# First loads by quarters of D, and half of the first token block transposed by DMA, in a GeGLU feed-forward kernel

## Chip, cores and metric

One core of one Trainium2 chip. The metric is the device time of one execution in microseconds (us). A verdict is a ratio: the mean time of one kernel's fast runs over the mean of the other's fast runs of the same rounds, so it is not quite the ratio of the medians that are quoted beside it. Beside the time each run has a span, from the first to the last instruction, which is 1.7 to 2.6 us shorter (mostly 1.8) and excludes what lies around the program.

## The reference

```python
B, S, D, F = 1, 2048, 1024, 3584      # bf16 inputs
def reference(x, w_gate, w_up, w_down):
    return (gelu(x @ w_gate) * (x @ w_up)) @ w_down    # gelu: tanh approximation
```

## The kernel before

The kernel works on two halves of the tokens. D lies on the partitions for the first two products, so x is needed transposed, as `xT`, in 8 tiles (kd = 0 to 7) of 128 rows of D; a token block is 512 tokens. The first 512 columns of w_gate and w_up (four groups of 128, "units") are done with 128 plain bf16 matmuls, the "first phase" here. All that follows is done in groups of seven products with prepared sums, the "second phase" (line 396, then 632); it keeps TensorE busy to the end.

The start of the first half, cut:

```python
XQ = 512; NSU = 3; NWARM = 11
load_x0_piece(0)                         # SP: 512 tokens x 512 of D, 512 KB
load_w((0, 0), 0, 2, nc.scalar)          # ACT: tiles 0,1 of w_gate, then w_up, 256 KB each
# ... 11 warm-up matmuls on constants ...
load_x0_piece(1)                         # SP: the other half of D
for k0 in range(2, 8, 2):
    load_w((0, 0), k0, k0 + 2, nc.sync)  # SP: tiles 2 to 7, full 512 columns
load_xT(xT, 0, 1, 0, KD)                 # SP: 2nd token block, one DMA transpose of 8 tiles
load_w((0, 1), 0, KD, nc.sync)           # SP: the next chunk of columns

def first_units(hT):
    # warm-up, 16 TensorE transposes (kd 0..3), then per kd six matmuls:
    # three units are held open at once; before kd = 3 the other 16 transposes
    ...
# then unit 3 of block 0, and units 0 to 3 of block 1, banks in rotation
```

Of the kernel before, what the change touches and what calls it, by code (L numbers as in the profile page):

```python
# [34 lines left out]
def kernel(  # L35
# [9 lines left out]
    P = 128  # L45
# [13 lines left out]
    DN = 512  # L59
    NDN = D // DN  # L60
    TSB = TB // P
    XQ = 512
    NXQ = D // XQ
    KPQ = XQ // P
    WKP = 2
    NSU = 3
    NWARM = 11
    NPAIR = KF // 2
    PPG = FPG // 2
    WDT = 2  # L70
# [36 lines left out]

    banks = [psum.tile([P, TB], F32, name=f"bank{i}") for i in range(8)]
    PB, VB, QB, RB = (0, 1), (2, 3), (4, 5), (6, 7)
    bank_ctr = [0]  # L110

    def next_bank():
        b = banks[bank_ctr[0] % 8]
        bank_ctr[0] += 1
        return b

    last_on = {}

    def on(engine, inst):
# [8 lines left out]
    def sp(inst):  # L128
        return on("sp", inst)
# [4 lines left out]
    def dve(inst):  # L134
        return on("dve", inst)
# [25 lines left out]
            for j in range(2)  # L161
        )

    def load_w(key, k0, k1, eng):
        c0 = key[1] * FG
        for w_sb, wv in zip(chunks[key], (wgv, wuv)):
            i = eng.dma_start(out=w_sb[:, k0:k1, :], in_=wv[:, k0:k1, c0 : c0 + FG])  # L167
            if eng is nc.sync:
                sp(i)

    def load_x0_piece(q):
        sp(
            nc.sync.dma_start(
                out=xs0[:, :, q * XQ : (q + 1) * XQ],
                in_=x2[0:TB, q * XQ : (q + 1) * XQ].rearrange(
                    "(ts p) d -> p ts d", p=P
                ),
            )
        )

    def load_xT(xT, h, tb, k0, k1):
        t0 = h * SH + tb * TB
        sp(
            nc.sync.dma_start_transpose(
                out=xT[:, k0:k1, tb * TB : (tb + 1) * TB],
                in_=xv[t0 : t0 + TB, k0:k1, :],
            )
        )

    xT = xT_pool.tile([P, KD, SH], BF16, name="xT")  # L190
    new_chunk((0, 0))
    load_x0_piece(0)
    load_w((0, 0), 0, WKP, nc.scalar)
    nc.scalar.preload_act_table(ACT.Gelu_apprx_tanh)
    ident = const_pool.tile([P, P], BF16, name="ident")
    make_identity(nc, ident[:])

    warm_l = nc.const_aps.tensor(1.0, [P, P], BF16)
    warm_r = nc.const_aps.tensor(1.0, [P, TB], BF16)
    warm = []  # L200
    for i in range(NWARM):
        b = banks[i % 8]
        warm.append(
            nc.tensor.matmul(b[:], lhsT=warm_l, rhs=warm_r, start=True, stop=True)
        )

    load_x0_piece(1)
    for k0 in range(WKP, KD, WKP):
        load_w((0, 0), k0, k0 + WKP, nc.sync)
    load_xT(xT, 0, 1, 0, KD)  # L210
    new_chunk((0, 1))
    load_w((0, 1), 0, KD, nc.sync)


    tsum = {}
# [25 lines left out]


    def mm_gu(ps, w_sb, fi, tb, kd):
        return nc.tensor.matmul(  # L244
            ps[:],
            lhsT=w_sb[:, kd, fi * P : (fi + 1) * P],
            rhs=xT[:, kd, tb * TB : (tb + 1) * TB],
            start=(kd == 0),
            stop=(kd == KD - 1),
        )  # L250

    g_ctr = [0]
# [19 lines left out]
            )  # L272
        )

    def unit(hT, key, fi, tb):
        pss = (next_bank(), next_bank())
        for ps, w_sb in zip(pss, chunks[key]):
            for kd in range(KD):
                mm_gu(ps, w_sb, fi, tb, kd)
        mult(hT, gelu(pss[0]), pss[1], key[1] * FPG + fi, tb)  # L280

    evac_ctr = [0]

    def evac(dst, src):
        if evac_ctr[0] % 2 == 0:
            dve(nc.vector.tensor_copy(out=dst, in_=src))
        else:
            act(nc.scalar.copy(out=dst, in_=src))
        evac_ctr[0] += 1

    def transpose_x_piece(q):
        kds = list(range(q * KPQ, (q + 1) * KPQ))
        parts = []
        if q == 0:
            parts = [([kds[0]], (0, 2)), ([kds[0]], (2, 4)), ([kds[1]], (0, 4))]
            kds = kds[2:]
        parts += [(kds[i : i + 2], (0, 4)) for i in range(0, len(kds), 2)]
        insts = []
        for kd_list, (ts0, ts1) in parts:
            n = (ts1 - ts0) * P  # L300
            tp = next_bank()[:].bitcast(BF16)
            for j, kd in enumerate(kd_list):
                for ts in range(ts0, ts1):
                    c = j * n + (ts - ts0) * P
                    insts.append(
                        nc.tensor.transpose(  # L306
                            tp[:, c : c + P],
                            xs0[:, ts, kd * P : (kd + 1) * P],
                            ident[:],
                        )  # L310
                    )
            k0 = kd_list[0]
            evac(
                xT[:, k0 : k0 + len(kd_list), ts0 * P : ts1 * P],
                tp[:, 0 : len(kd_list) * n].rearrange("p (a b) -> p a b", b=n),
            )
        return insts

    def first_units(hT):
        groups = [warm, transpose_x_piece(0)]  # L320
        held = [(banks[2 + 2 * u], banks[3 + 2 * u]) for u in range(NSU)]
        bank_ctr[0] = 0
        for kd in range(KD):
            if kd == KPQ - 1:
                bank_ctr[0] = 0
                groups.append(transpose_x_piece(1))
            g = []
            for j, w_sb in enumerate(chunks[(0, 0)]):
                g += [mm_gu(held[u][j], w_sb, u, 0, kd) for u in range(NSU)]
            groups.append(g)  # L330
        for ga, gb in zip(groups[:-1], groups[1:]):
            tc.add_manual_dep(
                gb[0].ins, ga[-1].ins.name, SCHED_DEP, reason="startup PE order"
            )
        t_sum("t1")
        for u in range(NSU):
            mult(hT, gelu(held[u][0]), held[u][1], u, 0)
        bank_ctr[0] = 0


    ssum = {}
# [434 lines left out]
    for h in range(NH):  # L776
        hT = hT_pool.tile([P, KF, SH], BF16, name="hT")
        first_pair = 0
        if h == 0:
            first_units(hT)  # L780
            t_sum("t2")
            for fi in range(NSU, FPG):
                unit(hT, (0, 0), fi, 0)
            t_sum("b22")
            t_sum("t3")
            unit(hT, (0, 0), 0, 1)
            for name in S_NAMES:
                for j in range(2):
                    s_sum(0, PPG, j, name)
            t_sum("t4")  # L790
            for fi in range(1, FPG):
                unit(hT, (0, 0), fi, 1)
            first_pair = PPG
            xs = [(tb, kd) for tb in range(NTB) for kd in range(KD)]
            stage_load(0)
            stage_load(1)
        for pair in range(first_pair, NPAIR):
            if pair % PPG == 0 and (pair // PPG + 1) * PPG < NPAIR:
                key = (h, pair // PPG + 1)
                if key not in chunks:  # L800
                    new_chunk(key)
                    load_w(key, 0, KD, nc.sync)
            then = {}
            if h == 0:

# [44 lines left out]
        if h + 1 < NH:  # L850
            nh = h + 1
            xT = xT_pool.tile([P, KD, SH], BF16, name="xT")

            def x_fill(k0, k1):
                src = x_dram[:, k0:k1, :]
                sp(nc.sync.dma_start(out=xT[:, k0:k1, :], in_=src))

            def w_fill(c, j):
                if j == 0:
                    new_chunk((nh, c))  # L860
                w_sb, wv = chunks[(nh, c)][j], (wgv, wuv)[j]
                for k0 in range(0, KD, KH):
                    src = wv[:, k0 : k0 + KH, c * FG : (c + 1) * FG]
                    sp(nc.sync.dma_start(out=w_sb[:, k0 : k0 + KH, :], in_=src))

            def s_fill(j, *names):
                for name in names:
                    s_sum(nh, 0, j, name, True)

            then0["m6"] = [  # L870
                lambda k0=k0: x_fill(k0, k0 + WKP) for k0 in range(0, KD, WKP)
            ]
            then1["m6"] = [lambda: w_fill(0, 0)]
            then1["m7"] = [lambda: w_fill(0, 1)]
            then1["m2"] = [
                lambda: s_fill(0, "s1"),
                lambda: s_fill(1, "s1"),
                lambda: s_fill(0, "s2"),
                lambda: s_fill(1, "s2"),
                lambda: s_fill(0, "s3"),  # L880
                lambda: s_fill(1, "s3"),
            ]
            then1["m3"] = [lambda: t_sum("t1")]
            then1["m4"] = [
                lambda: s_fill(0, "a22"),
                lambda: s_fill(1, "a22"),
                lambda: t_sum("b22"),
                lambda: t_sum("t2"),
                lambda: t_sum("t3"),
                lambda: s_fill(0, "s4"),  # L890
                lambda: s_fill(1, "s4"),
                lambda: t_sum("t4"),
                pool_behind_dve,
                lambda: [w_fill(1, j) for j in range(2)],
            ]
# [32 lines left out]
```

## Time and profile before

| | before |
|---|---|
| time, median of 6 runs | 545.12 us (544.7 to 546.16) |
| span of the profiled run | 542.7 us |
| TensorE busy | 99% of the span |
| first real matmul | 6.41 us |
| second phase starts | 35.53 us |

The prediction below shows the chain and the timeline, columns start, length, engine, line, what. Two more lines, of the list of waits (who waited, for whom: us in total, times, longest), first 40 us:

```profile
PE bank L244 <- DMA w_mem<-in_w_up_dram: 0.4, 1, 0.4
...
SPq L184 <- DMA w_mem<-in_w_up_dram: 1.5, 1, 1.5
```

The first is TensorE's only wait after its first matmul. The second is the load queue on SP: before it issues the DMA transpose of line 184 it waits for an earlier load of w_up to land. The dates fit eight completion semaphores used in turn, so that a DMA waits for the one eight places before it; this is inferred from which loads are waited for. One line of the timeline, columns start, length, engine, line, what:

```profile
37.22 4.03 PE L396 MATMUL bank<-t_mem,s_mem 128*128 128x512 f32 x16
```

The second phase's first eight plain matmuls start at 35.53, and the first product with prepared sums at 37.22 us, 1.69 us later.

### The profile page before, as it was taken

The numbers are of one execution on the slowest core, as the hardware profiler recorded it, in microseconds if no ns is written. First come the engines' busy times: TensorE is split into PE (matmuls) and PEld (weight loads), VectorE is DVE, ScalarE is ACT, GpSimd is POOL, SyncE is SP. The second block draws the span as 40 slices with busy tenths as digits, with TensorE's granted clock in tenths as the row PEclk, the third lists the DMA queues.
The fourth block names the chain that finished last, engine by engine and source line by source line (L and its number), as shares of the span: only waits on it lengthen the run. The fifth ranks groups of instructions, "written<-read, shape, count | busy, mean of one in ns | idle before, by whom it ended". The sixth has DMA issues, their size and how long they took to land.

```text
span 542.7 us, 7261 instructions
## 1 busy us (share of the span) xinstructions
PE 537.7 (99%) x2411; PEld 374.1 (69%) x2411; DVE 349.5 (64%) x465; ACT 259.8 (48%) x434; POOL 242.2 (45%) x206
## 2 busy tenths in 40 slices
PE   8999999999999999999999999999999999999997
PEld 4456677777767676767777766777766776866865
DVE  1826666778766899789484444444454469979961
ACT  2435555555555318216455555555555552462270
POOL 0577777888877000000038776677777630000000
PEclk9999999999999999999999999999999999999999
DMA  9845598877736979679962240404040457767845
GB/s 275 267 133 155 162 241 278 216 252 194 252 137 213 335 246 367 215 245 307 320 213 80 76 129 27 155 2 156 0 156 0 156 171 238 251 219 246 289 146 206
DMA packets 81669, 104.82 MB, mean 193 GB/s; under 512 B 16608, under 2 KB 63200, under 8 KB 81632
## 3 DMA queue, kind: packets, MB, share of 16 engines
q1 hardware_dynamic: 81088, 103.83, 60.0%
q10 hardware_dynamic: 544, 0.52, 0.3%
q8 instruction: 20, 0.33, 0.2%
q14 instruction: 17, 0.14, 0.1%
HBM read 87.56 MB, written 13.63 MB: 186 GB/s over the span
## 4 chain that ended last, share of the span: by engine, by line
PE 98%; DMA 1%; ACT 0%; ACTq 0%; issue 0%
PE bank L396 60%; PE bank L632 32%; PE bank L244 5%; DMA w_mem<-in_w_up_dram 1%; PE bank L306 0%; ACT o_sb L680 0%; ACTq L167 0%; ACTq L680 0%
## 5 line engine op out<-in xcount | busy, mean ns | idle before, releaser
L396 PE MATMUL bank<-t_mem,s_mem 128*128 128x512 f32 x1016 | 249.2, 399 | 0.0
L396 PEld LDWEIGHTS bank<-t_mem,s_mem 128*128 128x128 f32 x1016 | 190.9, 188 | 44.2
L370 POOL TENSOR_TENSOR s_mem<-w_mem 128x512 fp32r<-128x512 bf16 x100 | 120.9, 1230 | 196.1 <-DVE t_mem L238 105.0
L632 PE MATMUL bank<-t_mem,s_mem 128*128 128x512 f32 x560 | 130.1, 392 | 0.0
L419 DVE TENSOR_TENSOR bank<-bank,m 128x512 f32<-128x512 f32 x104 | 72.3, 699 | 81.3 <-ACT bank L439 72.3
L632 PEld LDWEIGHTS bank<-t_mem,s_mem 128*128 128x128 f32 x560 | 105.2, 188 | 22.7
L267 DVE TENSOR_TENSOR hT<-w_mem,bank 128x512 bf16<-128x512 f32 x104 | 71.3, 688 | 54.4 <-ACT w_mem L262 24.6
L262 ACT ACTIVATE w_mem<-bank 128x512 f32<-128x512 f32 x104 | 61.9, 597 | 79.4 <-DVE bank L419 46.2
L396 PE MATMUL bank<-xT,w_mem 128*128 128x512 bf16 x416 | 99.0, 380 | 0.0
L396 PEld LDWEIGHTS <-w_mem 128*128 128x128 bf16 x416 | 36.6, 98 | 50.5 <-issue 13.6
L545 DVE TENSOR_TENSOR t_mem<-w_mem 128x1024 fp32r<-128x1024 bf16 x56 | 65.5, 1216 | 0.0
L370 POOL TENSOR_TENSOR s_mem<-w_mem,s_mem 128x512 fp32r<-128x512 bf16 x50 | 63.3, 1288 | 0.0
L370 POOL TENSOR_TENSOR s_mem<-s_mem,w_mem 128x512 fp32r<-128x512 f32 x50 | 59.3, 1206 | 0.0
L607 DVE TENSOR_TENSOR s_mem<-hT 128x512 fp32r<-128x512 bf16 x56 | 40.5, 754 | 10.5 <-PE bank L632 7.0
L383 ACT CAST s_mem<-w_mem 128x512 fp32r<-128x512 bf16 x52 | 31.9, 615 | 30.4 <-PE bank L396 29.2
L632 PEld LDWEIGHTS <-hT 128*128 128x128 bf16 x224 | 21.3, 98 | 26.6 <-issue 1.8
L434 ACT COPY m<-bank 128x512 f32<-128x512 f32 x52 | 30.6, 589 | 17.2 <-PE bank L396 17.0
L439 ACT COPY bank<-bank 128x512 f32<-128x512 f32 x52 | 29.6, 570 | 17.1 <-PE bank L396 17.1
L430 ACT COPY bank<-bank 128x512 f32<-128x512 f32 x52 | 29.5, 570 | 13.4 <-PE bank L396 13.4
L680 ACT CAST o_sb<-bank 128x512 bf16<-128x512 f32 x28 | 15.4, 586 | 39.6 <-PE bank L632 39.6
L244 PE MATMUL bank<-xT,w_mem 128*128 128x512 bf16 x128 | 28.1, 379 | 0.4 <-DMA w_mem<-in_w_up_dram 0.4
L542 ACT CAST t_mem<-w_mem 128x1024 fp32r<-128x1024 bf16 x28 | 26.9, 1048 | 0.0
(39 smaller groups left out, 233.4 us busy)
## 6 DMA issues: line engine op xcount, KB each, us to landing
t_mem<-t_dram SPq DMA_DIRECT2D x56, 512.0 KB, 5.5
w_mem<-in_w_gate_dram SPq DMA_DIRECT2D x11, 1024.0 KB, 6.2
w_mem<-in_w_up_dram SPq DMA_DIRECT2D x11, 1024.0 KB, 8.4
wd_sb<-in_w_down_dram SPq DMA_DIRECT2D x28, 256.0 KB, 3.4
t_dram<-o_sb SPq DMA_DIRECT2D x28, 256.0 KB, 2.5
wd_sb<-in_w_down_dram SPq DMA_DIRECT2D x12, 512.0 KB, 8.5
w_mem<-in_w_down_dram SPq DMA_DIRECT2D x10, 512.0 KB, 5.8
w_mem<-in_w_down_dram SPq DMA_DIRECT2D x4, 1024.0 KB, 6.8
```

The source lines that it names most:

```text
L244: return nc.tensor.matmul(ps[:], lhsT=w_sb[:, kd, fi * P : (fi + 1) * P], rhs=xT[:, kd, tb * TB : (tb + 1) * TB], start=(kd == 0), stop=(k ...
L262: act(nc.scalar.activation(out=g_sb, in_=ps[:], func=ACT.Gelu_apprx_tanh))
L267: nc.vector.tensor_tensor(out=hT[:, fc, tb * TB : (tb + 1) * TB], in0=g_sb, in1=ps[:], op=ALU.mult,)
L370: pool(nc.gpsimd.tensor_tensor(out=t, in0=in0, in1=in1, op=op))
L383: act(nc.scalar.copy(out=t, in_=a(1, 1)))
L396: nc.tensor.matmul(banks[bank][:], lhsT=lhs[:, c, :], rhs=rhs[:, c, :], start=start and c == 0, stop=c == KH - 1, skip_group_check=True,)
L419: nc.vector.tensor_tensor(out=banks[dst][:], in0=banks[src][:], in1=m5[j][:], op=ALU.add)
L434: act(nc.scalar.copy(out=m5[j][:], in_=banks[VB[j]][:]))
L439: act(nc.scalar.copy(out=banks[RB[j]][:], in_=banks[QB[j]][:]))
L545: dve(nc.vector.tensor_tensor(out=t, in0=in0, in1=in1, op=ALU.subtract))
L607: dve(nc.vector.tensor_tensor(out=t, in0=in0, in1=in1, op=op))
L632: nc.tensor.matmul(banks[bset[u]][:], lhsT=lhs(i, u), rhs=rhs(i), start=start and i == 0, stop=stop and i == NS - 1, skip_group_check=True,)
```

## The change

The intent is to let TensorE begin sooner: a quarter of x and half the weight columns are enough for the first matmuls, and half of the transposing is taken off TensorE. The rest of the diff keeps instruction order fixed on each engine and changes which PSUM banks the first units use. The diff, cut to its core:

```diff
-    XQ = 512
+    XQ = 256
-    NSU = 3
-    NWARM = 11
+    NWARM = 8
@@ loads
-    load_x0_piece(0)
-    load_w((0, 0), 0, WKP, nc.scalar)
+    FA = 2 * P                                  # 256 of the 512 columns
+    load_x0(0, sp)                              # 256 KB
+    load_w(first, 0, 0, 2, act, 0, FA)          # w_gate, 128 KB
+    load_w(first, 1, 0, 2, sp, 0, FA)           # w_up
+    load_x0(1, act)
+    load_w(first, 0, 2, 4, sp, 0, FA)
+    load_w(first, 1, 2, 4, act, 0, FA)
@@ after the warm-up
-    load_x0_piece(1)
-    for k0 in range(WKP, KD, WKP):
-        load_w((0, 0), k0, k0 + WKP, nc.sync)
-    load_xT(xT, 0, 1, 0, KD)
+    for j in range(2):
+        load_w(first, j, KH, KD, sp, 0, FA)
+    for kd in range(KH, KD):
+        load_xT(xT, 0, 0, kd, kd + 1)           # four DMA transposes, block 0
+    for j in range(2):
+        load_w(first, j, 0, KD, sp, FA, FG)     # the other 256 columns
+    for k0 in range(0, KD, KH):
+        load_xT(xT, 0, 1, k0, k0 + KH)
@@ first units: two held instead of three; 8 transposes, 6 matmuls,
@@ 8 transposes, 26 matmuls; then units 2 and 3, then block 1, whose
@@ last unit now ends in banks VB, not PB
```

"Columns" below are the loads of the other 256 columns.

More of the change, by code (lines that the diff above doesn't have):

```diff
@@ L109 @@
     PB, VB, QB, RB = (0, 1), (2, 3), (4, 5), (6, 7)
-    bank_ctr = [0]
-    def next_bank():
-        b = banks[bank_ctr[0] % 8]
-        bank_ctr[0] += 1
-        return b
     last_on = {}
@@ L162, in new_chunk, with load_w, load_x0 @@
         )
-    def load_w(key, k0, k1, eng):
+    def load_w(key, j, k0, k1, queue=sp, f0=0, f1=FG):
         c0 = key[1] * FG
-        for w_sb, wv in zip(chunks[key], (wgv, wuv)):
-            i = eng.dma_start(out=w_sb[:, k0:k1, :], in_=wv[:, k0:k1, c0 : c0 + FG])
-            if eng is nc.sync:
-                sp(i)
-    def load_x0_piece(q):
-        sp(
-            nc.sync.dma_start(
-                out=xs0[:, :, q * XQ : (q + 1) * XQ],
-                in_=x2[0:TB, q * XQ : (q + 1) * XQ].rearrange(
-                    "(ts p) d -> p ts d", p=P
-                ),
-            )
-        )
+        eng = nc.scalar if queue is act else nc.sync
+        src = (wgv, wuv)[j][:, k0:k1, c0 + f0 : c0 + f1]
+        queue(eng.dma_start(out=chunks[key][j][:, k0:k1, f0:f1], in_=src))
+    def load_x0(q, queue):
+        eng = nc.scalar if queue is act else nc.sync
+        cols = slice(q * XQ, (q + 1) * XQ)
+        src = x2[0:TB, cols].rearrange("(ts p) d -> p ts d", p=P)
+        queue(eng.dma_start(out=xs0[:, :, cols], in_=src))
     def load_xT(xT, h, tb, k0, k1):
@@ L191 @@
     new_chunk((0, 0))
-    load_x0_piece(0)
-    load_w((0, 0), 0, WKP, nc.scalar)
-    nc.scalar.preload_act_table(ACT.Gelu_apprx_tanh)
+    FA = 2 * P
+    first = (0, 0)
+    load_x0(0, sp)
[4 more added lines that the diff above has]
+    load_w(first, 1, 2, 4, act, 0, FA)
+    act(nc.scalar.preload_act_table(ACT.Gelu_apprx_tanh))
     ident = const_pool.tile([P, P], BF16, name="ident")
@@ L199 @@
     warm_r = nc.const_aps.tensor(1.0, [P, TB], BF16)
-    warm = []
     for i in range(NWARM):
-        b = banks[i % 8]
-        warm.append(
-            nc.tensor.matmul(b[:], lhsT=warm_l, rhs=warm_r, start=True, stop=True)
-        )
-    load_x0_piece(1)
-    for k0 in range(WKP, KD, WKP):
-        load_w((0, 0), k0, k0 + WKP, nc.sync)
-    load_xT(xT, 0, 1, 0, KD)
+        pe(
+            nc.tensor.matmul(
+                banks[i][:], lhsT=warm_l, rhs=warm_r, start=True, stop=True
+            )
+        )
+    for j in range(2):
[6 more added lines that the diff above has]
+        load_xT(xT, 0, 1, k0, k0 + KH)
     new_chunk((0, 1))
-    load_w((0, 1), 0, KD, nc.sync)
+    for j in range(2):
+        load_w((0, 1), j, 0, KD)
     tsum = {}
@@ L243, in mm_gu @@
     def mm_gu(ps, w_sb, fi, tb, kd):
-        return nc.tensor.matmul(
-            ps[:],
-            lhsT=w_sb[:, kd, fi * P : (fi + 1) * P],
-            rhs=xT[:, kd, tb * TB : (tb + 1) * TB],
-            start=(kd == 0),
-            stop=(kd == KD - 1),
+        pe(
+            nc.tensor.matmul(
+                ps[:],
+                lhsT=w_sb[:, kd, fi * P : (fi + 1) * P],
+                rhs=xT[:, kd, tb * TB : (tb + 1) * TB],
+                start=(kd == 0),
+                stop=(kd == KD - 1),
+            )
         )
@@ L273, in mult, with unit_out, unit @@
         )
-    def unit(hT, key, fi, tb):
-        pss = (next_bank(), next_bank())
-        for ps, w_sb in zip(pss, chunks[key]):
+    def unit_out(hT, bset, fi, tb):
+        mult(hT, gelu(banks[bset[0]]), banks[bset[1]], fi, tb)
+    def unit(hT, bset, fi, tb):
+        for b, w_sb in zip(bset, chunks[first]):
             for kd in range(KD):
-                mm_gu(ps, w_sb, fi, tb, kd)
-        mult(hT, gelu(pss[0]), pss[1], key[1] * FPG + fi, tb)
-    evac_ctr = [0]
-    def evac(dst, src):
-        if evac_ctr[0] % 2 == 0:
-            dve(nc.vector.tensor_copy(out=dst, in_=src))
-        else:
-            act(nc.scalar.copy(out=dst, in_=src))
-        evac_ctr[0] += 1
@@ L291, in transpose_x_piece @@
-    def transpose_x_piece(q):
-        kds = list(range(q * KPQ, (q + 1) * KPQ))
-        parts = []
-        if q == 0:
-            parts = [([kds[0]], (0, 2)), ([kds[0]], (2, 4)), ([kds[1]], (0, 4))]
-            kds = kds[2:]
-        parts += [(kds[i : i + 2], (0, 4)) for i in range(0, len(kds), 2)]
-        insts = []
-        for kd_list, (ts0, ts1) in parts:
-            n = (ts1 - ts0) * P
-            tp = next_bank()[:].bitcast(BF16)
-            for j, kd in enumerate(kd_list):
-                for ts in range(ts0, ts1):
-                    c = j * n + (ts - ts0) * P
-                    insts.append(
-                        nc.tensor.transpose(
-                            tp[:, c : c + P],
-                            xs0[:, ts, kd * P : (kd + 1) * P],
-                            ident[:],
-                        )
-                    )
-            k0 = kd_list[0]
-            evac(
-                xT[:, k0 : k0 + len(kd_list), ts0 * P : ts1 * P],
-                tp[:, 0 : len(kd_list) * n].rearrange("p (a b) -> p a b", b=n),
-            )
-        return insts
@@ L319, in first_units @@
-    def first_units(hT):
-        groups = [warm, transpose_x_piece(0)]
-        held = [(banks[2 + 2 * u], banks[3 + 2 * u]) for u in range(NSU)]
-        bank_ctr[0] = 0
-        for kd in range(KD):
-            if kd == KPQ - 1:
-                bank_ctr[0] = 0
-                groups.append(transpose_x_piece(1))
-            g = []
-            for j, w_sb in enumerate(chunks[(0, 0)]):
-                g += [mm_gu(held[u][j], w_sb, u, 0, kd) for u in range(NSU)]
-            groups.append(g)
-        for ga, gb in zip(groups[:-1], groups[1:]):
-            tc.add_manual_dep(
-                gb[0].ins, ga[-1].ins.name, SCHED_DEP, reason="startup PE order"
-            )
-        t_sum("t1")
-        for u in range(NSU):
-            mult(hT, gelu(held[u][0]), held[u][1], u, 0)
-        bank_ctr[0] = 0
+                mm_gu(banks[b], w_sb, fi, tb, kd)
@@ new lines, in unit, with transpose_x0 @@
+        unit_out(hT, bset, fi, tb)
+    def transpose_x0(q):
+        parts = [(2 * q, 0, 4), (2 * q + 1, 0, 4)]
+        if q == 0:
+            parts = [(0, 0, 2), (0, 2, 4), (1, 0, 4)]
+        for n, (kd, ts0, ts1) in enumerate(parts):
+            tp = banks[(PB + QB)[(2 * q + n) % 4]][:].bitcast(BF16)
+            for ts in range(ts0, ts1):
+                pe(
+                    nc.tensor.transpose(
+                        tp[:, ts * P : (ts + 1) * P],
+                        xs0[:, ts, kd * P : (kd + 1) * P],
+                        ident[:],
+                    )
+                )
+            cols = slice(ts0 * P, ts1 * P)
+            if n % 2 == 0:
+                dve(nc.vector.tensor_copy(out=xT[:, kd, cols], in_=tp[:, cols]))
+            else:
+                act(nc.scalar.copy(out=xT[:, kd, cols], in_=tp[:, cols]))
@@ new lines, in first_units @@
+    def first_units(hT):
+        wg, wu = chunks[first]
+        held = (VB, RB)
+        transpose_x0(0)
+        for q in range(NXQ):
+            for kd in (2 * q, 2 * q + 1):
+                for u in range(2):
+                    mm_gu(banks[held[u][0]], wg, u, 0, kd)
+            for kd in (2 * q, 2 * q + 1):
+                for u in range(2):
+                    mm_gu(banks[held[u][1]], wu, u, 0, kd)
+                if kd == 0:
+                    transpose_x0(1)
+        for u in range(2):
+            unit_out(hT, held[u], u, 0)
@@ L780 @@
             first_units(hT)
+            unit(hT, PB, 2, 0)
+            t_sum("t1")
+            unit(hT, QB, 3, 0)
             t_sum("t2")
-            for fi in range(NSU, FPG):
-                unit(hT, (0, 0), fi, 0)
             t_sum("b22")
+            unit(hT, VB, 0, 1)
             t_sum("t3")
-            unit(hT, (0, 0), 0, 1)
             for name in S_NAMES:
@@ L789 @@
                     s_sum(0, PPG, j, name)
+            unit(hT, RB, 1, 1)
             t_sum("t4")
-            for fi in range(1, FPG):
-                unit(hT, (0, 0), fi, 1)
+            unit(hT, QB, 2, 1)
+            unit(hT, VB, 3, 1)
             first_pair = PPG
@@ L801 @@
                     new_chunk(key)
-                    load_w(key, 0, KD, nc.sync)
+                    for j in range(2):
+                        load_w(key, j, 0, KD)
             then = {}
@@ L860, in w_fill @@
                     new_chunk((nh, c))
-                w_sb, wv = chunks[(nh, c)][j], (wgv, wuv)[j]
                 for k0 in range(0, KD, KH):
-                    src = wv[:, k0 : k0 + KH, c * FG : (c + 1) * FG]
-                    sp(nc.sync.dma_start(out=w_sb[:, k0 : k0 + KH, :], in_=src))
+                    load_w((nh, c), j, k0, k0 + KH)
             def s_fill(j, *names):
```

## The prediction

> **What bounds the kernel now.** I read the page's busy table first, then the chain of waits with its list in order of time, then the timeline of the first 37 us, and last the DMA rate in 1 us stretches.
>
> ```profile
> PE 537.7 (99%) x2411; PEld 374.1 (69%) x2411; DVE 349.5 (64%) x465; ACT 259.8 (48%) x434; POOL 242.2 (45%) x206
> PE 98%; DMA 1%; ACT 0%; ACTq 0%; issue 0%
> ```
>
> TensorE is busy 99% of the span and is 98% of the chain that ended last: nothing but matmul time counts. The chain in order of time shows the only place where something else sets the end:
>
> ```profile
> 1.24 6.36 DMA w_mem<-in_w_up_dram
> 7.60 0.05 issue
> 7.65 3.41 PE bank L244 x15
> 11.06 0.89 PE bank L306 x16
> 11.95 23.74 PE bank L244 x110
> 35.70 151.35 PE bank L396 x672
> ```
>
> From 7.65 us on TensorE never stops; 110 matmuls in 23.74 us are 0.2158 us each. The start is 7.65 us of waiting for a first piece of w_up, with few matmuls before it. The timeline shows what TensorE and the load queue do there:
>
> ```profile
> 0.77 4.42 PE L204 MATMUL bank<-const-bfloat16-1.0 128*128 128x512 bf16 x11 [0.77 <-PEq L912]
> 5.51 1.07 PE L306 MATMUL bank<-ident,w_mem 128*128 128x128 bf16 x16 [0.32 <-DMA w_mem<-in_x_dram]
> 6.41 0.82 PE L244 MATMUL bank<-xT,w_mem 128*128 128x512 bf16 x3
> 7.62 6.00 SPq L184 DMA_TRANSPOSE xT<-in_x_dram  x1
> 7.65 3.41 PE L244 MATMUL bank<-xT,w_mem 128*128 128x512 bf16 x15 [0.41 <-DMA w_mem<-in_w_up_dram]
> 10.90 1.06 PE L306 MATMUL bank<-ident,w_mem 128*128 128x128 bf16 x16
> 35.53 2.04 PE L396 MATMUL bank<-xT,w_mem 128*128 128x512 bf16 x8
> ```
>
> Eleven warm-up matmuls, 16 transposes, three matmuls, a wait, then the stream. The first phase (the 128 plain matmuls of the first weight chunk) gives way to the second at 35.53 us. Only that date can move. From there to the end, some 507 us, the loop is untouched and has no wait.
>
> The DMA side, columns: stretch, length, busy time of PE, PEld, DVE, ACT, POOL, clock, DMA share, GB/s:
>
> ```profile
> 2.00:3.00 1.00, 1.00 (x4) 0.44 (x3) 0.00 (x0) 1.00 (x1) 0.00 (x0) 1.00 0.74 225
> 8.00:9.00 1.00, 1.00 (x7) 0.44 (x5) 0.00 (x0) 0.00 (x0) 0.00 (x0) 1.00 1.10 347
> 14.00:15.00 1.00, 1.00 (x6) 0.44 (x5) 0.00 (x0) 0.00 (x0) 0.00 (x0) 1.00 1.27 290
> ```
>
> Bytes flow from about 2 us on, then at 347 GB/s for plain pieces and 290 GB/s while x is transposed; the engines are full until 15.5 us. So the start is a race between fixed bytes and TensorE, and what counts is the order of the bytes.
>
> **What the Trainium skill says.** "TensorE: Matmul & The Clock Gate", section "Wait — 56ns, not 53.3ns?": 512-column matmuls start every 426.7 ns cold and every 215.7 ns warm, 128-column ones every 55.6 ns warm. The trace agrees: 0.2158 us per matmul, 0.89 us for 16 transposes, and warm-up weight loads 0.43 us apart until about 4.6 us. The same page, "What's actually happening": full clock comes after a busy window of about 3.4 us. The trace agrees roughly: warm-up began at 0.77 us and the spacing shortened at about 4.7 us. "DMA: Bandwidth & Descriptors", "Issuing engines are not separate DMA queues": a second issuing engine saves sequencer time only. The trace agrees that the total stays near 350 GB/s with both queues at work (between 4 and 8 us one moved 1.11 MB, the other 0.35). The same page, "Latency and other measured facts": 261 GB/s effective for a DMA transpose; the trace has 290.
>
> **The change part by part.**
>
> Warm-up: 8 instead of 11. 8 x 0.427 = 3.4 us, so it ends at 4.2 us instead of 5.2. It saves only if x is there by then.
>
> First x: a quarter of D, 256 KB instead of 512 KB. In the kernel before, 512 KB on the SP queue were usable at 5.5 us, when that queue had moved 0.78 MB, so landing trails the bytes by about 0.8 us. The queue had moved 0.08 MB at 2.5 us and then 0.23 MB per us. It passes 256 KB at about 3.2 us, so the piece is usable at about 4.1 us, as the warm-up ends. The first w_gate piece is 128 KB instead of 256 KB, on the ACT queue (0.11 MB per us): about 3.8 us. Both are in time.
>
> Transposes on TensorE: 16 instead of 32, in two sets of 8. The instruction order of the changed kernel puts 8 before the first matmul and 8 after the sixth. 16 x 0.056 = 0.9 us of TensorE time goes. First matmul: transposes at 4.25, plus half a tile transposed and copied by ScalarE (0.37 us for 128x256). In the kernel before, that ScalarE copy ended at 6.31 after a start at 5.51, so the first matmul could not come before 0.8 us; hence 5.1 us here instead of 6.41.
>
> Without any wait the first phase then ends at 5.1 + 128 x 0.2158 + 8 x 0.056 = 33.2 us, which is 2.4 us before 35.53. This is the ceiling.
>
> Now the waits. With no stall TensorE wants, by the same 0.2158: the second x quarter at 6.4, w_up of tiles 2 and 3 at 8.1, the four DMA-transposed tiles of x at 8.9, 9.4, 10.7 and 11.1, the other half of the columns of w_gate at 12.4 and of w_up at 14.1, and the second token block at 19.3 us.
> - Second x quarter: it ends 384 KB on the ACT queue, 2.5 + 0.36/0.11 = 5.8 us; about in time. w_up tiles 2 and 3: 512 KB on that queue, about 7.3 us; in time.
> - DMA transposes: SP issues five loads first (about 0.5 us each), then each transpose must find its completion semaphore free, which the order view shows as a wait on an earlier load (the second x quarter for the third transpose, about 6 us). In the long loop a one-tile transpose holds the SP queue 1.16 us at least, 1.67 us in the median, 4.19 us at most. From 4.0 us, four at 1.2 to 1.7 end between 8.8 and 10.8 us. Landing took 2.6 us at least, and 1.5 MB of loads ahead of them drain until about 7 us. Estimate: tiles at about 8.6, 9.8, 11.2 and 12.3 against 8.9, 9.4, 10.7 and 11.1. The last is late by some 1.2 us.
> - Other column half: issued only behind the transposes, at 9 to 11 us; about 1.4 us to first bytes (0.74 to 2.1 at the start), 1.5 us for 512 KB, 0.8 us to land: 12.7 to 14.7 against 12.4. Late by 0.3 to 2.3, largely the same wait as the one before, not added to it.
> - Second token block: two issues of 3 us (half of the 6.00), landed by about 18 to 19; in time.
>
> I book 1.0 us of wait for the transposes and columns. The clock may still be half for the transposes and first matmuls; 0.1 us more is for that. 2.4 - 1.1 = 1.3 us gained: 545.26 - 1.3 = 543.9 us.
>
> **The rivals.**
> - The ceiling: transposes land in time and the whole 2.4 us stay, 542.9 us. For it: 1.16 us issues exist, and the sizes look matched to these dates. Against: eight tiles in one instruction took 6.00 us to issue and 8.2 to land, with the DMA full.
> - The DMA transpose becomes the new wait: at 2 to 2.6 us per issue, as in the loop just behind two 1 MB loads (a pair took 5.19 us), the last tile is there at about 14 us and the columns at about 16. The gain is gone: 545 to 546.5 us.
> - The clock is not released after only 3.4 us of warm-up, and 3.4 us more of half speed follow: some 8 matmuls lost, 1.7 us, so about 545.5 us. Against: all work follows without a gap if x lands at 4.1.
> - GpSimd becomes the bound. It waits for the second weight chunk (20.24 us before) and makes the sums that TensorE wants 1.9 us into the second phase. Now the chunk is issued at 16 to 17 us instead of 13.67, landing at about 23 and 25. GpSimd had finished its first two pairs 10.5 us after its start, and the second pair is wanted at about 38 us, so some 3 us of slack stay. Otherwise the second phase stalls a few us. I give this little.
>
> **Range and chances.** Ceiling 542.9 with 0.3 us for run to run (544.74 to 545.34 before): low end 542.6. All the gain lost: 545.4. A change of 2% is 10.9 us; the whole start is 7.65 us of waiting, so faster by 2% cannot be, and slower would need waits three times any estimate above. Faster 0.005, within 0.985, slower 0.01.
>
> **What would show it.** Right: warm-up ends at about 4.2, first real matmul near 5.1, 16 identity matmuls in all, and TensorE's second phase starting near 34.2 with gaps totalling about 1 us, each ended by a DMA of xT or w_gate before 15 us. Wrong: a first matmul after 5.6 (landing is not set by bytes), transposes holding SP over 2 us each, matmul spacing of 0.43 us after 5.2, or a wait of TensorE for s_mem near 36 us.

## The result, and the profile after

| | before | predicted | changed |
|---|---|---|---|
| time, median | 545.12 us | 543.9 us | 543.59 us (543.35 to 543.98, 6 runs) |
| ratio | | | 0.9971 (0.9958 to 0.9984) |
| span of the profiled run | 542.7 | | 541.7 us |
| x usable, first transpose | 5.51 | 4.1 to 4.25 | 4.76 us |
| first real matmul | 6.41 | 5.1 | 5.62 us |
| identity matmuls | 32 | 16 | 16 |
| time of the first phase after that without matmul or transpose | 0.60 | 1.0 | 0.98 us |
| second phase starts | 35.53 | 34.2 | 34.67 us |

"Same", by the 2% rule, and a small gain clear of noise. The timeline of the changed kernel, cut, as the prediction shows it for the kernel before:

```profile
0.77 3.28 PE L197 MATMUL bank<-const-bfloat16-1.0 128*128 128x512 bf16 x8 [0.77 <-PEq L898]
4.50 5.12 SPq L172 DMA_TRANSPOSE xT<-in_x_dram  x4
4.76 0.62 PE L295 MATMUL bank<-ident,w_mem 128*128 128x128 bf16 x8 [0.70 <-DMA w_mem<-in_x_dram]
5.62 1.46 PE L245 MATMUL bank<-xT,w_mem 128*128 128x512 bf16 x6 [0.24 <-ACT xT L305]
7.36 5.80 PE L245 MATMUL bank<-xT,w_mem 128*128 128x512 bf16 x25
13.87 20.96 PE L245 MATMUL bank<-xT,w_mem 128*128 128x512 bf16 x94 [0.72 <-DMA w_mem<-in_w_gate_dram]
34.67 1.89 PE L381 MATMUL bank<-xT,w_mem 128*128 128x512 bf16 x8
36.21 4.00 PE L381 MATMUL bank<-t_mem,s_mem 128*128 128x512 f32 x16
```

Read the brackets. TensorE waits for x (0.70), for ScalarE's copy of the transposed half tile (0.24), and then at 13 us for w_gate: the columns. (A bracket counts from the modelled end of the matmul before, which lies some 0.17 us after the date at which the next could have started. By start times, 7.36 + 26 x 0.2158 = 12.97, so this wait is 0.90 us; the brackets of the other runs below are short by as much. The program has 26 matmuls there; the record misses one.) There is no wait for a DMA-transposed tile. The last two lines are 1.54 us apart, 0.15 less than before. The chain of waits in order of time (start, us, what; steps of 0.02 to 0.05 us left out) says where the columns' date comes from:

```profile
0.74 3.74 DMA w_mem<-in_w_gate_dram
4.50 1.22 SPq L172
5.76 1.24 SPq L172
7.05 1.26 SPq L172
8.35 1.26 SPq L172
9.66 4.17 DMA w_mem<-in_w_gate_dram
13.87 9.52 PE bank L245 x43
```

SP waits 3.74 us for the first w_gate piece (its semaphore is wanted by the first DMA transpose), then spends 1.22 to 1.26 us on each of four transposes, only then issues the columns, and they land 4.17 us later. From there TensorE has 96 matmuls to do: 13.87 + 96 x 0.2158 = 34.6 us. The end of the first phase is set by a queue, not by how soon TensorE began. The DMA engines had room meanwhile; stretch, length, PE, PEld, DVE, ACT, POOL, clock, DMA share, GB/s:

```profile
5.00:6.00 1.00, 0.76 (x9) 0.49 (x7) 0.72 (x2) 0.37 (x1) 0.00 (x0) 1.00 1.21 290
...
10.00:11.00 1.00, 1.00 (x6) 0.46 (x5) 0.00 (x0) 0.00 (x0) 0.00 (x0) 1.00 0.45 100
```

Full from 3 to 9 us, at 100 GB/s between 10 and 11.

**The books of the profiled pair.** First matmul 0.79 us sooner; eight transposes fewer behind it, 0.45 (16 before, 8 after). What is left of the first phase after the first matmul, when 128 x 0.2158 and the transposes are taken off, is 0.60 us before (35.53 - 6.41 - 27.62 - 0.90) and 0.98 after (34.67 - 5.62 - 27.62 - 0.45), 0.38 more. So the second phase starts 0.79 + 0.45 - 0.38 = 0.86 us sooner. The bank order gives another 0.15. Sum 1.0, the difference of the spans (542.7 and 541.7). The medians of time differ by 1.5 us; the rest is not explained and is taken up below.

### The profile page after: what moved, and what is told of

Same layout as the page of the kernel before. It is cut to its first block, busy times and chain, and to the rows that moved or that the text cites. A ratio compares the mean times of both kernels' runs of the same rounds, so it can differ in the third digit from the quotient of the medians.

```text
span 541.7 us, 7194 instructions
## 1 busy us (share of the span) xinstructions
PE 533.9 (99%) x2356; PEld 372.6 (69%) x2392; DVE 350.5 (65%) x465; ACT 258.4 (48%) x433; POOL 239.5 (44%) x206
## 4 chain that ended last, share of the span: by engine, by line
PE 96%; DMA 1%; SPq 1%; issue 0%; ACT 0%; ACTq 0%
PE bank L381 60%; PE bank L617 32%; PE bank L245 4%; DMA w_mem<-in_w_gate_dram 1%; SPq L172 1%; ACT o_sb L665 0%; ACTq L665 0%
## 5 line engine op out<-in xcount | busy, mean ns | idle before, releaser
L355 POOL TENSOR_TENSOR s_mem<-w_mem 128x512 fp32r<-128x512 bf16 x100 | 117.4, 1194 | 197.7 <-DVE t_mem L238 103.3
L381 PE MATMUL bank<-xT,w_mem 128*128 128x512 bf16 x391 | 97.5, 380 | 1.3
L381 PEld LDWEIGHTS <-w_mem 128*128 128x128 bf16 x416 | 36.6, 98 | 50.4 <-issue 13.1
L245 PE MATMUL bank<-xT,w_mem 128*128 128x512 bf16 x125 | 28.1, 379 | 1.1 <-DMA w_mem<-in_w_gate_dram 0.7
```

The lines of the kernel that those rows point to most:

```text
L245: nc.tensor.matmul(ps[:], lhsT=w_sb[:, kd, fi * P : (fi + 1) * P], rhs=xT[:, kd, tb * TB : (tb + 1) * TB], start=(kd == 0), stop=(kd == KD ...
L355: pool(nc.gpsimd.tensor_tensor(out=t, in0=in0, in1=in1, op=op))
L381: nc.tensor.matmul(banks[bank][:], lhsT=lhs[:, c, :], rhs=rhs[:, c, :], start=start and c == 0, stop=c == KH - 1, skip_group_check=True,)
```

## The experiments

Theory 1: the SP queue's issue time sets the columns' date, and this date the end of the first phase; what TensorE saves before it is hidden. Theory 2: the bytes ahead in the DMA engines set the dates, whatever queue issues them. A third possibility comes from the prediction's sum: every part saved counts by itself. Twelve kernels ran, all correct, four at a time on one chip: e1 to e4 on the first, e5, e6, e9 and e10 on the second, e7, e12, a1 and a2 on the third. The kernel before had median spans of 542.7, 542.9 and 543.3 us there. The changed kernel unaltered ran on the third alone (a1), so spans of runs on different chips are compared by their difference to the kernel before on the same chip, in brackets below.

| run | edit to the changed kernel | second phase | median span (to before, same chip) | ratio to before |
|---|---|---|---|---|
| e1 | columns issued by ACT | 35.45 | 542.45 (-0.25) | 0.9999 |
| e2 | one load fewer ahead of the transposes | 33.74 | 541.2 (-1.5) | 0.9968 |
| e3 | one DMA transpose of four tiles | 34.24 | 541.0 (-1.7) | 0.9969 |
| e4 | no DMA transpose in block 0 | 34.92 | 541.8 (-0.9) | 0.9978 |
| e5 | 11 warm-up matmuls | 34.70 | 541.65 (-1.25) | 0.9976 |
| e6 | (kernel before) 8 warm-up matmuls | 36.58 | 543.65 (+0.75) | 1.0016 |
| e9 | 4 warm-up matmuls | 35.50 | 542.5 (-0.4) | 0.9994 |
| e10 | e2 and e3 together | 34.34 | 541.3 (-1.6) | 0.9973 |
| a1 | none | 34.47 | 541.6 (-1.7) | 0.9968 |
| a2 | e2 again | 33.79 | 541.2 (-2.1) | 0.9964 |
| e7 | x's first quarter split over both queues | 35.50 | 542.9 (-0.4) | 0.9993 |
| e12 | e2 with 9 warm-up matmuls | 34.22 | 541.1 (-2.2) | 0.9966 |

The intervals of the ratios are 0.0012 to 0.0017 to each side, so ratios 0.0010 apart are not told apart by time. The second phase's date is read to 0.01 us, but from one profile of each run: the changed kernel itself gave 34.67 and, in a1, 34.47.

### e1: columns from the ACT queue

```diff
-    for j in range(2):
-        load_w(first, j, 0, KD, sp, FA, FG)
@@ first_units, behind transpose_x0(1)
+                    for j in range(2):
+                        load_w(first, j, 0, KD, act, FA, FG)
```

> Only edit to the changed kernel: the loads of the second column half of w_gate and w_up are issued from the ACT queue behind its last copy of the start (about 8.2 us), not from SP behind the four one-tile DMA transposes (9.66 and 10.28 us). Theory 1 (the SP queue's issue time sets the wait): w_gate's half lands at 12.7 to 13.0 us instead of 13.87, TensorE's waits of 0.72 and 0.38 us go, the second phase starts at about 33.8 us instead of 34.67, and the time falls by 0.8 to 1.0 us against the changed kernel (ratio to before about 0.9955 instead of 0.9971). Rival, theory 2 (the bytes ahead set it): landing, waits and time stay as they are, 34.6 us and 0.997.

It missed, both ways. The columns were issued at 8.23 and 9.21 us, as meant, but the second phase came 0.8 us later, at 35.45. The chain of e1:

```profile
7.98 5.42 DMA xT<-in_x_dram
...
13.44 22.18 PE bank L243 x102
```

The last tile of x, issued at 7.98 us, now took 5.42 us to land, and TensorE waited 1.78 us for it. Between 8.0 and 13.4 us the ACT queue moved 0.85 MB and the SP queue 0.39 MB: the columns went past the tile. So taking a load out of the SP queue put it in the way of what stayed there. (In the changed kernel that tile was issued at 8.35 us and landed 2.7 us later.) The columns themselves landed at 13.1 us, 0.7 sooner, though issued 1.4 sooner. Theory 1 fits the wait that went, theory 2 the new one. The edit also let SP issue the transposes of the second block earlier, from about 9.3 instead of 10.91 us; no run separates their bytes from those of the columns.

### e2: one load fewer ahead of the transposes

```diff
-    load_w(first, 1, 2, 4, act, 0, FA)
+    load_w(first, 1, 2, KD, act, 0, FA)
@@
-    for j in range(2):
-        load_w(first, j, KH, KD, sp, 0, FA)
+    load_w(first, 0, KH, KD, sp, 0, FA)
```

> Only edit to the changed kernel: tiles 2 to 7 of w_up's first columns are one load on the ACT queue, so one load fewer stands ahead of the DMA transposes and the first of them need not wait for a completion semaphore (1.2 us, 3.3 to 4.5 us). Theory 1: transposes start at about 2.8 to 3.3 us instead of 4.50, the column half is issued at about 8.5 us instead of 9.66, its wait goes, second phase at about 33.8 us; w_up's tiles 2 and 3 now land later (about 8.5 us, wanted at 8.7), which may give back up to 0.5 us. Theory 2: no change, 34.6 us.

As theory 1 said: second phase at 33.74 us, and the list of waits has none of TensorE after its first matmul until 270 us. The chain shows the columns issued at 8.54 instead of 9.66 us and landing in about the same time:

```profile
4.19 1.12 SPq L172
...
5.36 1.83 SPq L172
...
7.23 1.26 SPq L172
...
8.54 4.35 DMA w_mem<-in_w_gate_dram
...
12.93 20.97 PE bank L244 x96
```

It still runs through the columns: TensorE could have gone on at 7.04 + 26 x 0.2158 = 12.65 us and was released at 12.93. So their date sets the end here too, now by only 0.28 us.

But the span of this profile was 541.7 us, the changed kernel's. The timeline shows where most of the 0.93 us went:

```profile
272.07 1.85 PE L616 MATMUL bank<-t_mem,s_mem 128*128 128x512 f32 x7 [0.63 <-DMA t_mem<-t_dram]
```

A load issued at 263.97 us took 7.97 us to land instead of a median 5.3 and TensorE waited 0.63 us, in code that nothing here touches. The changed kernel's profile has no wait there.

### e3: one DMA transpose of four tiles

```diff
-    for kd in range(KH, KD):
-        load_xT(xT, 0, 0, kd, kd + 1)
+    load_xT(xT, 0, 0, KH, KD)
```

> Only edit to the changed kernel: the four upper tiles of x come by one DMA transpose of four tiles instead of four of one. Theory 1: it holds the SP queue about 3 us (half of the 6.00 of eight tiles) instead of 5.1, so the column half is issued at about 7.5 us and is in time; the first of the four tiles, wanted at 9.5 us, is usable only when all have landed, about 9.5 to 10, so a new wait of 0 to 0.5 us; second phase at 33.7 to 34.2 us. Theory 2: no change, 34.6 us.

As theory 1 said, at the late end: the columns were issued at 8.07 us and were in time; TensorE waited 0.40 us for the tiles instead; second phase at 34.24. SP was held 3.74 us, not 3. The wait in the timeline:

```profile
10.07 24.33 PE L244 MATMUL bank<-xT,w_mem 128*128 128x512 bf16 x112 [0.40 <-DMA xT<-in_x_dram]
```

In this profile, too, TensorE waited for the t_mem loads near 272 us (0.95 us in two pieces), and it was the slowest of its five runs: span 542.8 against 540.9 to 541.1 of the others.

### e4: no DMA transpose in block 0

```diff
-    for kd in range(KH, KD):
-        load_xT(xT, 0, 0, kd, kd + 1)
+    for q in (2, 3):
+        load_x0(q, sp)
@@
-                if kd == 0:
-                    transpose_x0(1)
+                if kd == 2 * q and q + 1 < NXQ:
+                    transpose_x0(q + 1)
```

> Only edit to the changed kernel: the upper half of D of the first block is also loaded plain, by quarters, and transposed by TensorE; small pieces and order stay. Theory 1: 16 more transposes cost 16 x 0.056 = 0.9 us of TensorE, but the SP queue is free from about 4.5 us and the column waits (1.0 us) go: second phase at about 34.6 us, the same time as the changed kernel within 0.3 us, so the DMA transpose itself brought nothing net. Theory 2: the waits stay and 0.9 us are added: 35.5 us, as the kernel before.

Theory 1's number: 34.92 us, no wait after the first matmul, 16 more transposes on TensorE. So the DMA transpose in the title is worth 0.25 us of the second phase's date, or 0.45 against a1; by time it isn't resolved. What else was changed brings the rest: without the DMA transpose, 35.53 became 34.92. Small pieces, shorter warm-up and order are not separated in that.

### e5, e6 and e9: the warm-up

> Only edit to the changed kernel: 11 warm-up matmuls again. Theory 1 (after the start, the date of the columns alone sets the second phase; the first matmul's date is hidden by the wait at 13.2 us): the first matmul comes 0.2 to 0.7 us later, the wait for the columns shrinks by as much, second phase at 34.6 to 34.8 us and the time as the changed kernel's (ratio about 0.997). Rival (the savings of the prediction's sum add up, the shorter warm-up is a saving of its own): second phase 0.3 to 0.7 us later, 35.0 to 35.4 us, ratio about 0.998.

> The kernel before with 8 warm-up matmuls and nothing else. Theory 1: nothing is won, TensorE idles from 4.1 us until its 512 KB of x are usable at 5.5 us: second phase at 35.5 us, ratio 1.000 within 0.0005. Rival (the warm-up is a saving of its own): about 1 us earlier, ratio 0.998. A third way: the clock is lost over the gap of 1.3 us, transposes and matmuls run slower and the time rises by 0.5 us or more.

> The changed kernel with 4 warm-up matmuls: TensorE idles from 2.5 us until x lands at about 4.5 us. If the clock needs the busy 3.4 us before x (the rival of the prediction), the transposes are 0.107 us and the first matmuls 0.43 us apart until about 8 us, some 7 matmuls at 0.21 us extra: kd 0 to 3 end about 1.4 us later and use up the column wait, second phase at 35.1 to 35.5 us. If the clock comes on its own, nothing changes: 34.6 us.

The edits are `NWARM = 11` in the changed kernel, `NWARM = 8` in the kernel before, and `NWARM = 4` in the changed one. The timeline of e5:

```profile
6.51 1.56 PE L245 MATMUL bank<-xT,w_mem 128*128 128x512 bf16 x6
...
8.35 26.51 PE L245 MATMUL bank<-xT,w_mem 128*128 128x512 bf16 x122
```

The first matmul came at 6.51 us, 0.9 later than with 8 and as late as in the kernel before, yet the second phase stands at 34.70, as the changed kernel's. The wait for the columns has gone in exchange. Theory 1 is right and the sum of parts is not: the earlier first matmul, the aim of the change, was worth next to nothing here. It is 0.03 us against the changed kernel, and 0.23 against a1, which issued its first DMA transpose as early as e5 did (4.12 and 4.14 us; 4.50 in the changed kernel's profile). The cushion is just used up in e5: its columns landed at 13.6 us and TensorE reached them at 8.35 + 26 x 0.2158 = 13.96. By this reckoning a still later start would cost its full length. The line of e6 that matters:

```profile
5.44 1.89 PE L306 MATMUL bank<-ident,w_mem 128*128 128x128 bf16 x16 [1.09 <-DMA w_mem<-in_x_dram]
```

The next matmul started at 7.12 us, so the 16 transposes were 0.105 us apart, not 0.056: TensorE ran at half rate. The first matmul came 0.7 us later than with 11, and the second phase 1.05 us later. That is the third way of its expectation. In e9 the 8 transposes took 1.03 us and the first six matmuls 2.72 instead of 1.46; the second phase came at 35.50, in the expected range. All four executions of e6 had longer spans (543.5 to 544.2) than any of the kernel before on that chip (542.6 to 543.2).

The idle time alone does not explain a half rate: in a1, e5, e7 and e10 the first 8 transposes took 1.03 to 1.06 us with no wait before them, and in the changed kernel 0.62 us behind 0.70 us of idle. What sets e6 and e9 apart is when the rate rose. In e6 the 18 matmuls behind took 4.82 us instead of 18 x 0.2158 = 3.88, so some 4.5 of them ran at the warm-up's 0.43 us and the rate rose at about 9.0 us; the same working gives about 9.5 for e9, but at 6 to 6.7 us in those four runs and before 5.5 us in the kernel before. So a warm-up that ends 1.09 us or more before x is not a saving; why the date varies between runs with a longer one stays open.

### e10: e2 and e3 together

The edit is the sum of both diffs.

> The edits of e2 (one load fewer ahead) and e3 (one DMA transpose of four tiles) together. Theory 1: the transpose is issued at 2.8 us without a wait and holds the SP queue about 3.7 us, tiles usable at about 8.6 us (wanted at 9.2), columns issued at about 6.5 us, no wait for either: second phase at 33.7 us as in e2, not sooner, since TensorE is then bound by the first matmul at 5.3 us plus its own 28.5 us; ratio 0.996 to 0.9965, as far as the later wait for t_mem near 270 us of e2 and e3 lets it through.

A miss, and theory 2's. The chain of e3 and then of e10:

```profile
4.28 5.75 DMA xT<-in_x_dram
```

```profile
2.81 7.32 DMA xT<-in_x_dram
```

Issued 1.5 us sooner, the tiles landed at 10.1 us all the same, and the instruction held SP 5.36 instead of 3.74 us. That fits bytes ahead setting a transpose's date, with the queue setting only the loads behind it; no run varies those bytes by themselves. TensorE waited 0.36 us, the second phase stood at 34.34.

### a1, a2, e12 and e7

a1 is the changed kernel unaltered; a2 is e2 unaltered; e12 is e2 with `NWARM = 9`; e7 is

```diff
-    load_x0(0, sp)
+    # tokens 0..255 of the quarter on SP, tokens 256..511 on ACT, 128 KB each
```

> The changed kernel unaltered, for a comparison on the same chip as the other three. Second phase at 34.5 to 34.9 us, waits of about 1 us for the columns, ratio 0.997 to 0.9975.

> The kernel of e2 once more (one load fewer ahead of the DMA transposes). If the wait for t_mem near 270 us, which ate 0.6 of its 0.9 us, is chance, this profile may be without it and the spans lie 0.7 to 0.9 us below those of the changed kernel; if an earlier start brings it on, it is there again and the spans lie 0.2 to 0.5 us below. Second phase at 33.7 to 33.9 us in both cases.

> The kernel of e2 with 9 warm-up matmuls, so that TensorE has no gap of 0.3 us before x. If the gap is what lets the first transposes run slow in some executions, the 8 transposes take 0.45 us and the second phase stands at 33.7 to 33.9 us in all; if the clock depends on the moment alone, there is no gain, and the ninth warm-up matmul costs up to 0.2 us. Time as e2 within 0.3 us.

> The changed kernel with the first quarter of x cut into two halves of 128 KB, first on each of both queues; it tests the step of the prediction that was 0.3 to 0.6 us off, the date at which x is usable (4.1 forecast, 4.4 to 4.76 seen). If sharing the engines with the other queue's w_gate piece made x late, x is usable 0.3 us sooner, about 4.1 us, with w_gate later; if the first bytes and the landing set it, it stays at 4.4 to 4.7. By theory 1 the second phase does not gain from it: the loads and transposes behind find their semaphores later, so 34.6 to 35.1 us.

a1 shows the cushion once more, by chance. Its timeline:

```profile
4.37 1.03 PE L295 MATMUL bank<-ident,w_mem 128*128 128x128 bf16 x8
5.43 1.97 PE L245 MATMUL bank<-xT,w_mem 128*128 128x512 bf16 x6
...
7.69 5.79 PE L245 MATMUL bank<-xT,w_mem 128*128 128x512 bf16 x25
13.68 20.95 PE L245 MATMUL bank<-xT,w_mem 128*128 128x512 bf16 x94 [0.20 <-DMA w_mem<-in_w_gate_dram]
```

Here the clock came late (transposes 1.03 us, six matmuls 1.97) and TensorE was 0.33 us behind the other profile at 7.7 us; the columns came at 13.68, their wait was 0.20, and the second phase stood at 34.47.

a2: second phase 33.79, no wait at 270 us, span 540.8 in the profile, but 540.6 to 541.6 over five runs. So the late wait comes in some executions of e2 and not in others. On this chip e2 lies 0.4 us below the changed kernel by median span, about half of what its start gains; by time the intervals overlap.

e12: transposes at full rate (0.61), but so they were in e2 and a2 with the gap (0.62), so it says nothing on the gap. The columns, issued at 8.56 us, took 4.9 us to land instead of 4.3 and TensorE waited 0.58 us. No gain over e2; the landing time differed by half of what e2's start gained, with the loads unchanged.

e7: x was usable before the warm-up ended (its halves landed 2.7 and 2.9 us after issue, at 3.4 and 3.6 us, instead of 4.4 to 4.76). That agrees with the other queue's piece making x late. But the second quarter then came late:

```profile
8.31 0.62 PE L298 MATMUL bank<-ident,w_mem 128*128 128x128 bf16 x8 [1.23 <-DMA w_mem<-in_x_dram]
```

Everything behind moved too, the columns to 14.76 us, and the second phase to 35.50, worse than the 34.6 to 35.1 that was expected.

## Why the prediction was right

- **What can move.** Right: TensorE has no wait from the second phase on, and its length was 507.2 us before and 507.0 after. Only the date of the second phase moved, and 0.15 us behind it.
- **First x at 4.1 us.** Too early by 0.3 to 0.65 us: 4.76 and 4.37 in the two profiles. The step assumed the queue shares and the rate of the kernel before. With 512-byte rows the two queues moved 323 GB/s between 2.5 and 4.5 us with the ACT queue taking 0.28 of 0.65 MB, where the forecast gave it a third; and only 0.03 MB had moved by 2.5 us, not 0.08. e7 fits the sharing as a cause. The first w_gate piece was late too, 4.48 us where 3.8 was forecast (that figure left out the 0.8 us of landing), and the first DMA transpose waited for it (1.2 us); the prediction had such a wait at the third transpose.
- **First matmul at 5.1 us.** 5.62, for that reason, and so past the 5.6 that the prediction named as a sign of being wrong (5.43 in a1). e5 shows that the error hardly mattered: with 6.51 the end was 0.03 to 0.23 us later.
- **The waits, 1.0 us.** The size was right (0.98, of it 0.90 for the columns), the larger part of the reason was not. The prediction booked it for a last tile of x 1.2 us late, with the columns largely in the same wait. But no tile was waited for: they landed at 9.0, 9.5, 9.9 and 11.1 us where 8.6, 9.8, 11.2 and 12.3 were forecast, and TensorE, 0.5 us late itself, wanted them later. Each transpose held SP 1.25 us, the low end of the 1.2 to 1.7 assumed. The columns' dates (issued 9.66, landed 13.87) lie in the forecast 9 to 11 and 12.7 to 14.7.
- **The sum.** Its total was close by luck in part. It forecast the second phase 1.3 us sooner; the profiles have 0.86, another 0.15 that was not foreseen, and the 0.5 by which the medians differ more than the profiled pair is not explained. (Its rounding is loose, too: 35.53 minus 33.2 is 2.3, not 2.4.) The sum treats the ceiling and the waits as separate terms; the chain shows one term, the columns' landing plus 96 matmuls, and e5 that what comes before is nearly all hidden under it.
- **The rivals.** The ceiling of 33.2 was not reached; e2 came nearest (33.74). A wait of TensorE for a DMA-transposed tile came in e1, e3 and e10, not in the change. Half rate at the first transposes was seen (e6, e9, and a1, e5, e7, e10), and in a1 was absorbed by the columns' wait. GpSimd never held TensorE: no wait of TensorE for s_mem in any of these profiles.
- **Not foreseen:** 0.15 us from the bank order. Before, VectorE still read the last unit's result until 36.49 us from a bank that the second phase starts with, and TensorE's next weight load for it came at 36.55.
- **Left open.** The profiled pair differs by 1.0 us, the medians by 1.5, and on the third chip the median spans by 1.7 (543.3 and 541.6). There nine runs of the kernel before spread from 542.8 to 543.7, five of the changed one from 541.4 to 541.7. It would fit that the columns' wait absorbs the variation of the clock and of the first landing, as a1 does, while before each such delay went through to the end, as e6's did. The profile of the kernel before may then be a fortunate one: it had the full rate before 5.5 us, where e5, with as many warm-up matmuls, had it at about 6.7. No run shows it execution by execution. Nor is it settled why a t_mem load is sometimes late (near 264 us in e2 and e3, near 506 us in e6).

No version beat the changed kernel by more than the intervals. By median span on the same chip, e12 (541.1) and a2 (541.2) lie below a1 (541.6). e2 and e3 had no changed kernel beside them; against the kernel before they gained 1.5 and 1.7 us, as a1 did (1.7).

## What to carry to other kernels

When a kernel is 99% one engine, ask of a change in its start which single date the rest hangs on, and compute the end from that date plus the work left; savings ahead of it do not add. A DMA transpose held the issuing queue 1.1 to 1.9 us for one tile and 2.3 to 5.4 us for four here, and what stood behind it in that queue paid; but moving that load to another queue made a tile that was being waited for 2.7 us slower to land (e1). A warm-up that ended 1.1 us or more before the first data (e6, e9) cost time.

## What the Trainium skill lacked or had wrong

- "DMA: Bandwidth & Descriptors" gives no issue time measured on trn2 for a DMA transpose beside busy engines. Here: 1.12 to 1.88 us of the SP queue for one tile of 128x512 (1.22 to 1.26 in the changed kernel), 3.74 us for four in one instruction with the engines busy, 5.36 us for the same instruction issued 1.5 us sooner, 6.00 for eight.
- The same page, "Issuing engines are not separate DMA queues", says that a second issuing engine only saves sequencer time. In e1, one run, it seems also to have changed who came first: a transposed tile issued at 7.98 us landed 5.42 us later while the other queue moved 0.85 of 1.25 MB.
- The same page, "Specifications", gives 512 bytes as enough for line rate. With the engines full, 512-byte rows moved at 290 to 327 GB/s here (3 to 6 us of the changed kernel), 1 KB rows at 347 to 379 (4 to 11 us of the kernel before); the two stretches differ in the mix of the queues as well.
